# The first 230 microseconds of a delta-rule and feed-forward kernel: weight transfers, score blocks and one unit's keys in another order

## The chip, the cores and the metric

One core of one Trainium2 chip runs the kernel. The metric is device time in microseconds (us), the median of several runs; lower is better. The engines are called PE (TensorE, matmuls), DVE (VectorE), ACT (ScalarE), POOL (GpSimd) and SP (SyncE, which only issues transfers here).

## The reference, cut to what matters

The first half is a delta-rule recurrence for 4 batches (B), 8 heads (H), 768 positions (S) and head size 48 (D). Its output, with the heads side by side, is the input x (3072 rows of 384) of a feed-forward block with a hidden size of 2048.

```python
k_n = k / (np.linalg.norm(k, axis=-1, keepdims=True) + 1e-06)
for t in range(S):
    y[:, :, t] = np.einsum('bhd,bhde->bhe', q[:, :, t], state)
    v_old = np.einsum('bhde,bhd->bhe', state, kt)
    state = state + bt[:, :, :, None] * np.einsum('bhd,bhe->bhde', kt, vt - v_old)
...
h = x @ w_in
g = h * (1.0 / (1.0 + np.exp(-1.702 * h)))
return g @ w_out
```

The two weight matrices come as 64-bit floats and are made 32-bit on the chip.

## The kernel before, in words

**Units.** The sequence is cut into 6 chunks of 128 positions; a unit is one chunk of one batch with all 8 heads, so there are 24 units, units 0 to 3 in chunk 0, 4 to 7 in chunk 1, and so on. For each unit the keys are normalised (`normalize_mixed`, line 317: a square on ACT, a sum on DVE, a power on POOL, three instructions on DVE), turned (`turn`, 385: matmuls into psT, copied by ACT to kT), and their scores formed (`gram`, 362: matmuls into psG, copied by ACT to G). The 32-row diagonal blocks of the scores are written to a DRAM tile Nd and read back into NT so that each of 128 partitions holds one block (`prepare`, 389). `invert` (444) inverts these blocks for a whole chunk on DVE, from `NT*bI` (bI is beta) to YS; YS goes out to Yd in DRAM and comes back as XB. `Step` (538) then solves a unit in four blocks, one after the other: psU (solve, with XB), a copy of U on ACT, psR (below), a subtraction from V on DVE. A "hop" is one call of `together` (786) on two units in turn. `put_out` (951) forms the output psY, updates the state ST on DVE, and copies the output to xT. Part of each xT tile is moved between partitions by six small transfers `xT<-last` (681 to 690).

**Weights.** w_in is fetched in four quarters (`fetch_in`, 174, twelve transfers each, of 64 and 192 KB), w_out in 16 pieces (`fetch_out`, 190). They land in parts of tiles that are otherwise free (w_out's own space, gT, xT, M). `conversions` (255) turns them into 32-bit floats, five DVE instructions and one ACT instruction for a piece; each `fill(n)` puts n more of these instructions at its place in the program. Fetches of later pieces are tied to the end of a conversion (283 to 291): the end of piece ("in", 0, 1) calls fetch_in(3), the end of ("in", 1, 1) calls four fetch_out on POOL's queue.

**Order.** Engines and queues work in the order in which the program gives them. `pinned` (100) keeps an instruction in program order; `sync`, `beside` and `other_queue` (115) are such transfers on the queues of SP, ACT and POOL. What isn't pinned (`nc.sync.dma_start`) is placed by the scheduler. Each transfer on SP's and ACT's queues uses one of eight completion counters in turn, and waits for the counter's last user.

**The beginning (871 to 1031).** Keys of chunk 0 are normalised and turned, and only their diagonal blocks formed (`diagonal`, 428), for two units at a time; Nd is read back into NT as one transfer (913). Behind it stand on SP: QP and V of units 0 to 3, fetch_in(1) (half of it on POOL's queue), KN of units 4 to 6, fetch_in(2), and bI of the other chunks. `invert(0)` runs on DVE meanwhile; at its end `warm(NY)` puts 60 small matmuls on PE, and YS and XB go through DRAM. Then units 0 and 1 hop (973 to 978), with `warm(NU)` of 11 matmuls in each hop, are put out, and units 2 and 3 hop (998 to 1006), with the first hidden-layer matmuls (ph) from the fourth hop on. `keys` (956) prepares units 4 to 7 in 26 small steps among these hops, at steps 0, 3, 6 and 14; `ahead_of(preparing, n)` takes n steps. After chunk 0, `invert(1)` runs on DVE among ph matmuls. Then `woven` (828) is called for each unit, with the keys of the unit five ahead, so those of unit 8 in woven(3). `follow` (802) loads QP, KN and V for later units.

Of the kernel before, what the change touches and what calls it, by code (L numbers as in the profile page):

```python
# [18 lines left out]
def kernel(  # L19
# [19 lines left out]
    nc = tc.nc  # L39

    B, H, S, D = q.shape
# [8 lines left out]
    BS = 32  # L50
    NB = C // BS
    HB = 2
# [5 lines left out]
    NW, NA, NY, NU = 80, 3, 60, 11  # L58
# [20 lines left out]
    NT = cpool.tile([128, BS, BS], F32, name="NT")  # L79
# [4 lines left out]
    def load(n, pairs, dma=nc.sync.dma_start):  # L84
        c, b = units[n]
        for dst, src in pairs:
            dma(  # L87
                out=dst[n % len(dst)][:, :, 0:D],
                in_=src[b, :, c * C : (c + 1) * C, :].rearrange("h p d -> p h d"),
            )  # L90

    def load_values(n, dma=nc.sync.dma_start):
        c, b = units[n]
        V = io.tile([128, H, D], F32, tag="V", name="V", bufs=4)
        dma(
            out=V, in_=v[b, :, c * C : (c + 1) * C, :].rearrange("h p d -> p h d")
        )
        loaded[n] = V
# [33 lines left out]
    def warm(n, after=None):  # L132
        ps = ps_moe.tile([128, 256], F32, tag="moe", name="ps_warm")
        if after is not None:
            after(ps[:, 0:1], 0.0)
        for _ in range(n):
            pe.matmul(ps, lhsT=ones[:, 0:128], rhs=ones, start=True, stop=True)
# [36 lines left out]
    def fetch_in(i, other=None):  # L174

        f = slice(i * NQ, (i + 1) * NQ)
        raw = quarter(i if i < 3 else 4)
        for j in range(KC):
            for p, r, m, step in x_rows:
                (other if other and p >= DP else sync)(  # L180
                    out=as_rows(raw[j])[p : p + m, 0],
                    in_=moe_w_in[r + j * step : r + j * step + m, f],
                )
# [110 lines left out]
    def fill(n):  # L294
        for _ in range(n):
            next(converting, None)
# [92 lines left out]
    def prepare(n):  # L389

        c, b = units[n]
        turn(n)
        yield 0.6
        G = gram(n)
        if c == 1:
            Nd = dram.tile([H * C * BS], F32, tag="Nd", name="Nd", bufs=4)
            for blk in range(NB):
                u = slice(blk * BS, (blk + 1) * BS)
                sync(out=Nd.rearrange("(h p k) -> p h k", p=C, k=BS)[u], in_=G[u, :, u])
            yield 0.9  # L400
            sync(
                out=NT[b * NB * H : (b + 1) * NB * H].rearrange("d i k -> d (i k)"),
                in_=Nd.rearrange("(d r) -> d r", r=BS * BS),
            )
            yield 0.0
            return
        Nd = dram.tile([H * NS], F32, tag="Nd", name="Nd", bufs=4)
        dma = sync if c < 3 else nc.sync.dma_start
        dma(
            out=Nd.rearrange("(h r) -> h r", r=NS)[:, 0 : C * C].rearrange(  # L410
                "h (p k) -> p h k", k=C
            ),
            in_=G,
        )
        dma(
            out=NT[b * NB * H : (b + 1) * NB * H],
            in_=Nd.rearrange("(d r) -> d r", r=NS // NB)[:, 0 : BS * C].rearrange(
                "d (i k) -> d i k", k=C
            )[:, :, 0:BS],
        )  # L420
        yield 0.9
# [116 lines left out]
    class Step:  # L538
# [126 lines left out]
        def outputs(self, state=False):  # L665
            self.turned(
                (0, 4, 1, 5, 2, 6, 3, 7),
                lambda h: self.US[:, h * D : h * D + DP], lambda h: self.M[:, h, :],
                self.c == 0,
            )  # L670
            if state:
                self.state(self.psS)
            t = slice(self.b % HB * C, (self.b % HB + 1) * C)
            if t.start == 0:
                lasts[0] = wk.tile([128, NTH], F32, tag="o", name="last")
            last = lasts[0]
            act.copy(last[:, t], self.psY[1][:, 1, :])
            act.copy(self.xT[:, 0::2, t], self.psY[0])
            act.copy(self.xT[:, 1, t], self.psY[1][:, 0, :])

            if t.start > 0:
                t, dmas = slice(0, NTH), [nc.sync.dma_start] * 2
                if self.c == 0:
                    dmas = [sync, beside if self.b < HB else sync]
                for ct in range(2):
                    for j in range(KC):
                        dmas[ct](
                            out=self.xT[ct * DP + D : (ct + 1) * DP, j, t],
                            in_=last[ct * DP + j * XR : ct * DP + (j + 1) * XR, t],
                        )  # L690
# [74 lines left out]
    def ahead_of(work, n):  # L765
        for _ in range(n):
            next(work, None)
# [33 lines left out]

    def follow(n):

        if n + B < len(units):
            load(n + B, ((QP, q),))
        m = n - 1 + len(KN)
        if m < len(units):
            load(m, ((KN, k),), nc.gpsimd.dma_start)
        if n - 1 + B < len(units):
            load_values(n - 1 + B)  # L810
        if n % HB == 0 and n > B:
            h = (n - 1) // HB
            gT = []
            queue.append(hidden(xTs[h], gT, slice(0, NTH), 1.3))
            queue.append(written(*units[h * HB], gT))
            xTs.pop(h)
# [7 lines left out]
            debt[0] -= done  # L824

    STEPS = (9, 5, 3, 3, 3, 3)

    def woven(n, share):

        nonlocal inverting
        A, B_, D_ = steps.pop(n - 1, None), steps.get(n), steps.get(n + 1) or NoStep()
        m = n + B + 1
        K = (normalize if n > 6 else normalize_mixed)(m) if m < len(units) else iter(())
        P = prepare(m) if m < len(units) else iter(())
        if n % HB == 1 and B < n and n + 1 + HB < len(units):
            inverting = invert(*units[n + 1 + HB], HB)
        ahead = STEPS[:3] if n % HB == 1 else STEPS[3:]  # L840

        next(K, None)
        together([(B_, 1)], [(A, 2)])
        run(D_.scored)
        next(K, None)
        ahead_of(inverting, ahead[0])
        spend(share / 3)

        together([(A, 3), (D_, 0)], [(B_, 1)])
        next(K, None)  # L850
        ahead_of(inverting, ahead[1])
        spend(share / 6)
        next(P, None)
        spend(share / 6)

        together([(B_, 2)], [(D_, 0)])
        if A:
            A.queries()
            A.outputs(True)
        run(P)  # L860
        ahead_of(inverting, ahead[2])
        if n % HB == 0:
            run(inverting)
        spend(share / 6)
        next(new_step(n + 2).scored, None)
        spend(share / 6)
        follow(n)
# [34 lines left out]
    for b in range(B):  # L902
# [4 lines left out]
        if b % 2 == 1:  # L907
            for e in range(2):
# [1 line left out]
                    out=Nd.rearrange("(h e p k) -> e p h k", e=2, p=C, k=BS)[e, :, (b - 1) * NP : (b + 1) * NP],  # L910
                    in_=Ds[e][:, b - 1 : b + 1].rearrange("p b h j -> p (b h) j"),
                )
    sync(out=NT.rearrange("d i k -> d (i k)"), in_=Nd.rearrange("(d r) -> d r", r=BS * BS))
    pool.tensor_copy(landed, NT[:, 0, 0:1])
    for b in range(B):
        load(b, ((QP, q),), sync)
    for b in range(B):
        load_values(b, sync)
    fetch_in(1, other_queue)
    for n in range(B, len(KN)):  # L920
        load(n, ((KN, k),), sync)
    fetch_in(2)
    for blk in range(NB):
        sync(out=bI[blk::NB, 1:], in_=betas[:, 1:, blk, :])
    fill(6)
    for b in range(B):
        gram(b)
# [10 lines left out]
    run(inverting)  # L938
    for s in pair:
        s.select()  # L940
    fill(5)

    def hops(a, b):
# [12 lines left out]
    def keys():  # L956

        def unit(n):
            yield from normalize_mixed(n)
            yield from prepare(n)  # L960

        work = [unit(n) for n in range(B, 2 * B)]
        for t in range(26):
            for u, begin in enumerate((0, 3, 6, 14)):
                s = t - begin
                if s >= 0 and s % 2 == 0:
                    next(work[u], None)
            yield
        for w in work:
            run(w)  # L970
# [8 lines left out]
    for s in pair[:2]:  # L979
        put_out(s)  # L980
        fill(1)
        ahead_of(preparing, 1)
    load(7, ((KN, k),), sync)
    for n in range(B, B + 2):
        load(n, ((QP, q),), sync)
    for n in range(B, B + 2):
# [4 lines left out]
    def feed(n=1):  # L991
        for _ in range(n):
            while ffn and next(ffn[0], None) is None:
                ffn.pop(0)
# [4 lines left out]
    for i in range(2 * NB):  # L999
        together(*next(path))  # L1000
        if i > 2:
            feed()
        fill(2)
        ahead_of(preparing, 2)
        if 3 <= i < 6:
            fetch_out(i - 3)
# [5 lines left out]
    xTs.pop(0), xTs.pop(1)  # L1012
    run(preparing)
    load(B + 2, ((QP, q),), sync)
    load(8, ((KN, k),), sync)
    while not ("in", 3, 1) in done:
        fill(1)
    inverting = invert(1)
# [47 lines left out]
```

## Time and profile before

| | us |
|---|---|
| median of 3 runs | 798.52 (792.38 to 800.28) |
| profiled execution, its own time | 793.2 |
| its span | 791.4 |
| busy in the span: PE, DVE, ACT, POOL | 759.3, 458.7, 239.7, 127.6 |
| mean granted PE clock | 0.974 |

A row of the timeline reads: start, duration, engine, line, operation, output<-input, shape and count, and in brackets the idle time of the engine before it and what ended that. Nearly all instructions carry line 102, the helper that pins them, so they are told apart by the names of their tiles. "SPq" and "ACTq" are the engines' queues: the time is that of issuing, not of moving the data. A row of the table by stage reads: stretch, its length, busy time and count for PE, PE's weight loads, DVE, ACT and POOL, then the granted PE clock, the DMA engines' mean share and GB/s.

### The profile page before, as it was taken

The numbers are of one execution on the slowest core, as the hardware profiler recorded it, in microseconds if no ns is written. First come the engines' busy times: TensorE is split into PE (matmuls) and PEld (weight loads), VectorE is DVE, ScalarE is ACT, GpSimd is POOL, SyncE is SP. The second block draws the span as 40 slices with busy tenths as digits, with TensorE's granted clock in tenths as the row PEclk, the third lists the DMA queues.
The fourth block names the chain that finished last, engine by engine and source line by source line (L and its number), as shares of the span: only waits on it lengthen the run. The fifth ranks groups of instructions, "written<-read, shape, count | busy, mean of one in ns | idle before, by whom it ended". The sixth has DMA issues, their size and how long they took to land.

```text
span 791.4 us, 18653 instructions
## 1 busy us (share of the span) xinstructions
PE 759.3 (96%) x8068; PEld 568.7 (72%) x8068; DVE 458.7 (58%) x945; ACT 239.7 (30%) x521; POOL 127.6 (16%) x128
## 2 busy tenths in 40 slices
PE   9678899898899999999999999999999999999998
PEld 7467788654568768768768778678678678687684
DVE  5897669897996566656666756766756531100000
ACT  4433553234333323323223223223223123121110
POOL 4122220101221312212212212211210000000000
PEclk9689799989999999999999999999999999999999
DMA  6996752343323232232232232231230020000000
GB/s 125 158 176 136 152 138 58 75 135 84 81 49 90 54 77 51 55 86 42 59 79 45 62 87 43 52 99 27 60 82 11 22 44 2 12 15 1 25 1 20
DMA packets 139313, 52.81 MB, mean 67 GB/s; under 512 B 113808, under 2 KB 134416, under 8 KB 139232
## 3 DMA queue, kind: packets, MB, share of 16 engines
q1 hardware_dynamic: 136864, 43.65, 25.6%
q0 software_dynamic: 2176, 7.67, 3.7%
q8 instruction: 63, 1.03, 0.6%
q10 hardware_dynamic: 192, 0.31, 0.2%
q14 instruction: 18, 0.15, 0.1%
HBM read 33.13 MB, written 17.30 MB: 64 GB/s over the span
## 4 chain that ended last, share of the span: by engine, by line
PE 82%; DVE 9%; SPq 3%; DMA 3%; issue 1%; ACT 1%; ACTq 0%; POOL 0%; DVEq 0%; POOLq 0%
PE ph L102 29%; PE po L102 28%; PE psY L102 6%; PE psU L102 5%; PE psQ L102 3%; PE psG L102 3%; SPq L102 3%; PE ps_warm L102 2%; DVE w_out L102 2%; PE psT L102 2%; PE psR L102 2%; DVE tmp L102 2%; DVE P L102 1%; DVE V L102 1%; DVE YB L102 1%
## 5 line engine op out<-in xcount | busy, mean ns | idle before, releaser
L102 PE MATMUL po<-w_out,gT 128*128 128x384 f32 x768 | 267.1, 496 | 4.9 <-DVE w_out L102 4.8
L102 PE MATMUL ph<-xT,w_in 128*128 128x256 f32 x1152 | 262.8, 384 | 0.5 <-ACT gT L102 0.2
L102 PEld LDWEIGHTS ph<-xT,w_in 128*128 128x128 f32 x1152 | 215.5, 191 | 33.5 <-ACT gT L102 1.6
L102 PEld LDWEIGHTS po<-w_out,gT 128*128 128x128 f32 x768 | 141.8, 191 | 96.2 <-DVE w_out L102 7.2
L102 DVE TENSOR_TENSOR V<-V,psR 64x384 f32<-64x384 f32 (+1 forms) x96 | 53.3, 556 | 198.9 <-PE psR L102 197.7
L102 ACT ACTIVATE gT<-ph 128x512 f32<-128x512 f32 x96 | 56.4, 596 | 137.8 <-PE ph L102 137.6
L102 DVE TENSOR_TENSOR P<-NT,YB 64x8 f32<-64x8 f32 (+31 forms) x190 | 88.5, 466 | 5.3
L102 ACT COPY US<-psU 32x384 f32<-32x384 f32 x92 | 43.2, 470 | 143.0 <-PE psR L102 127.3
L102 PEld LDWEIGHTS psU<-V,XB 32*32 32x32 f32 x1536 | 59.3, 107 | 36.8 <-issue 27.4
L102 DVE TENSOR_REDUCE YB<-P 64x4 f32<-64x8 f32 (+31 forms) x190 | 80.9, 426 | 6.5
L102 PE MATMUL psU<-V,XB 32*32 32x48 f32 x1536 | 70.2, 205 | 2.1 <-DMA XB<-Yd 1.4
L598 POOL TENSOR_SCALAR_AFFINE_SELECT M<-M 128x1024 f32<-128x1024 f32 x20 | 26.1, 1307 | 245.5 <-DVE M L102 166.6
L102 PE MATMUL psR<-US,G 32*32 32x48 f32 x2208 | 61.4, 205 | 0.6 <-issue 0.6
L102 PEld LDWEIGHTS psR<-US,G 32*32 32x32 f32 x2208 | 51.9, 107 | 1.9 <-issue 1.9
L102 PE MATMUL ps_warm<-ident 128*128 128x256 bf16 x260 | 38.0, 301 | 11.7 <-ACT G L102 7.2
L102 PEld LDWEIGHTS <-ident 128*128 128x128 bf16 x260 | 26.5, 106 | 18.3 <-issue 11.2
L102 PE MATMUL psQ<-QS,kT 48*128 48x176 f32 (+1 forms) x384 | 34.8, 322 | 1.1 <-ACT QS L102 1.1
L102 PE MATMUL psG<-kT 48*128 48x128 f32 x384 | 32.4, 316 | 2.7 <-ACT kT L102 2.5
L102 DVE TENSOR_TENSOR P<-NT 64x256 f32<-64x256 f32 (+7 forms) x40 | 33.7, 843 | 0.3
L102 DVE TENSOR_REDUCE NT<-P 64x64 f32<-64x1024 f32 (+7 forms) x40 | 32.6, 815 | 1.4
L87 POOL DMA_DIRECT2D KN<-in_k_dram x15 | 14.2, 949 | 117.2 <-PE psY L102 108.2
L102 PEld LDWEIGHTS psQ<-QS,kT 48*128 48x128 f32 x384 | 28.6, 192 | 4.0 <-ACT QS L102 2.4
(96 smaller groups left out, 610.5 us busy)
## 6 DMA issues: line engine op xcount, KB each, us to landing
Nd<-G SPq DMA_DIRECT2D x16, 512.0 KB, 3.5
QP<-in_q_dram SPq DMA_DIRECT2D x24, 192.0 KB, 3.8
V<-in_v_dram SPq DMA_DIRECT2D x24, 192.0 KB, 2.9
out_dram<-o SPq DMA_DIRECT2D x24, 192.0 KB, 2.5
XB<-Yd SPq DMA_DIRECT2D x24, 128.0 KB, 3.3
KN<-in_k_dram POOLq DMA_DIRECT2D x15, 192.0 KB, 3.9
Yd<-YS SPq DMA_DIRECT2D x22, 128.0 KB, 2.5
NT<-Nd SPq DMA_DIRECT2D x20, 128.0 KB, 2.6
```

Of the source, the lines that this page charges most:

```text
L87: dma(out=dst[n % len(dst)][:, :, 0:D], in_=src[b, :, c * C : (c + 1) * C, :].rearrange("h p d -> p h d"),)
L102: return lambda *a, **kw: tc.keep_in_program_order(op(*a, **kw))
L598: (pool if self.n < B else nc.gpsimd).affine_select(out=self.M, in_=self.M, compare_op=ALU.is_gt, fill=0.0, base=0, pattern=[[0, H], [1, 1 ...
```

## The change

- fetch_in(1) moves behind the KN loads and bI; fetch_in(2) moves behind the end of `invert(0)`, its transfers and the selections of units 0 to 3.
- Nd of chunk 0 is read back into NT in two halves of 64 partitions, each after its pair of units.
- The six `xT<-last` transfers of units 0 and 1 all go on SP (three were on ACT).
- In put_out of units 0 and 1 no step of `keys` is taken any more. The first three hops of units 2 and 3 get `warm(NU // 2)`, 5 matmuls each.
- Unit 8 is added to `keys` at step 17: it is normalised and turned there; its gram and its transfers stay in woven(3), which takes the begun `prepare` from `begun`.
- KN of unit 8 is loaded together with that of unit 7, before QP and V of units 4 and 5. On SP the loads KN 7, KN 8, QP 4, QP 5, V 4, V 5 now stand between the first six xT transfers and the first Nd of chunk 1; the last NT of chunk 1 stands behind the second six xT transfers (before it was ahead of them).
- In `follow`, for n up to 4, the loads of QP and V are pinned.

```diff
@@ outputs
                 if self.c == 0:
-                    dmas = [sync, beside if self.b < HB else sync]
+                    dmas = [sync, sync]
@@ follow
+        dma = sync if n <= B else nc.sync.dma_start
         if n + B < len(units):
-            load(n + B, ((QP, q),))
+            load(n + B, ((QP, q),), dma)
...
         if n - 1 + B < len(units):
-            load_values(n - 1 + B)
+            load_values(n - 1 + B, dma)
@@ woven
+    begun = {}
...
+        if m in begun:
+            K, P = iter(()), begun.pop(m)
@@ beginning
-    sync(out=NT.rearrange("d i k -> d (i k)"), in_=Nd.rearrange("(d r) -> d r", r=BS * BS))
-    pool.tensor_copy(landed, NT[:, 0, 0:1])
+            d = slice((b - 1) * NB * H, (b + 1) * NB * H)
+            sync(
+                out=NT[d].rearrange("d i k -> d (i k)"),
+                in_=Nd.rearrange("(d r) -> d r", r=BS * BS)[d],
+            )
+    pool.tensor_copy(landed[64:], NT[64:, 0, 0:1])
...
-    fetch_in(1, other_queue)
     for n in range(B, len(KN)):
         load(n, ((KN, k),), sync)
-    fetch_in(2)
     for blk in range(NB):
         sync(out=bI[blk::NB, 1:], in_=betas[:, 1:, blk, :])
+    fetch_in(1, other_queue)
...
     for s in pair:
         s.select()
+    fetch_in(2)
     fill(5)
@@ keys
-        work = [unit(n) for n in range(B, 2 * B)]
+        begun[2 * B] = prepare(2 * B)
+
+        def first(n):
+            yield from normalize_mixed(n)
+            next(begun[n])
+
+        work = [unit(n) for n in range(B, 2 * B)] + [first(2 * B)]
         for t in range(26):
-            for u, begin in enumerate((0, 3, 6, 14)):
+            for u, begin in enumerate((0, 3, 6, 14, 17)):
@@ put_out of units 0 and 1, hops of units 2 and 3
         fill(1)
-        ahead_of(preparing, 1)
     load(7, ((KN, k),), sync)
+    load(8, ((KN, k),), sync)
...
         if i > 2:
             feed()
+        else:
+            warm(NU // 2)
...
     load(B + 2, ((QP, q),), sync)
-    load(8, ((KN, k),), sync)
```

## The prediction

> **What bounds the kernel now.** First the page's row of slices: TensorE (PE) is busy nearly everywhere after the first third, so what can be won lies in its holes and in its slow stretches, and both stand in the first 230 us.
>
> ```profile
> PE   9678899898899999999999999999999999999998
> DVE  5897669897996566656666756766756531100000
> PEclk9689799989999999999999999999999999999999
> ```
>
> Slices are 19.8 us. PEclk falls to 0.6 in the second (the first inversion, on DVE) and to 0.7 in the fifth. Then the timeline between 48 and 90 us, at the end of the first inversion:
>
> ```profile
> 54.06 1.23 DVE L102 TENSOR_TENSOR YS<-YB,bI 128x1024 f32<-128x1024 f32 x1
> 54.15 8.03 PE L102 MATMUL ps_warm<-ident 128*128 128x256 bf16 x60 [3.05 <-DVE ps_warm L102]
> 54.91 2.62 SPq L102 DMA_DIRECT2D bI<-in_beta_dram  x4
> ...
> 57.63 1.00 SPq L102 DMA_DIRECT2D Yd<-YS  x2
> 57.64 0.85 ACTq L102 DMA_DIRECT2D Yd<-YS  x2
> ...
> 60.13 2.85 SPq L102 DMA_DIRECT2D XB<-Yd  x4
> ...
> 63.60 0.86 PE L102 MATMUL psU<-V,XB 32*32 32x48 f32 x16 [1.43 <-DMA XB<-Yd]
> ```
>
> YS is ready at 54.06+1.23 = 55.29, but SP is still issuing bI and starts the write of YS 2.34 us later. PE, whose 60 warm matmuls end at 62.18, waits another 1.43 us for XB. The chain of waits agrees: from 25 to 57.6 us it is SP's queue. The timeline of ACT and of PE after the first two units:
>
> ```profile
> 85.23 1.88 ACTq L102 DMA_DIRECT2D xT<-last  x3
> 87.16 0.60 ACT L102 ACTIVATE kT<-psT 128x512 f32<-128x512 f32 x1 [1.79 <-issue]
> ```
> ```profile
> 87.81 2.08 PE L102 MATMUL psG<-kT 48*128 48x128 f32 x16 [2.04 <-ACT kT L102]
> ```
>
> ACT issues three transfers, so kT is late and PE stands for 2.04 us. The table by stage shows what follows:
>
> ```profile
> 84.00:86.00 2.00, 1.77 (x34) 1.41 (x30) 1.56 (x3) 0.79 (x4) 2.00 (x3) 1.00 0.25 39
> 88.00:90.00 2.00, 2.00 (x27) 1.78 (x31) 0.00 (x0) 0.19 (x2) 0.00 (x0) 0.50 1.01 364
> 98.00:100.00 2.00, 2.00 (x5) 1.58 (x6) 1.93 (x4) 0.86 (x2) 0.00 (x0) 0.50 0.63 128
> ```
>
> (last three columns: granted clock, DMA share, GB/s). The clock is 0.50 until about 101: the hole costs its 2.04 us and then slow matmuls. Last, DVE and SP around the second inversion:
>
> ```profile
> 122.25 1.22 DVE L102 TENSOR_TENSOR NT<-NT,bI 128x1024 f32<-128x1024 f32 x1
> ...
> 154.03 0.55 DVE L102 TENSOR_REDUCE ssq<-ksq 128x8 f32<-128x384 f32 x1 [2.25 <-ACT ksq L102]
> ```
> ```profile
> 115.48 0.31 SPq L102 DMA_DIRECT2D NT<-Nd  x1
> 116.92 4.29 SPq L102 DMA_DIRECT2D xT<-last  x6
> ```
>
> From 116.4 to 190 DVE has one idle of note, the 2.25 us before unit 8's ssq; PE waits for it (4.8 us for w_out, 2.3 for KN). So until 190 the end is carried by PE to 116, then by DVE.
>
> **The Trainium skill.** "TensorE: Matmul & The Clock Gate", Part 1, "What's actually happening": the array drops to half rate after an idle window of about 3.4 us and needs as long of busy time to return. The trace agrees on the halves, not the lengths: 2.04 us sufficed, and 13 us passed. "DMA: Bandwidth & Descriptors", "Issuing engines are not separate DMA queues": another issuing engine only saves sequencer time. The trace agrees: three xT transfers cost ACT 1.88 us and SP 2.20. The same page, "Anatomy of one DMA": about 2 us of a transfer are fixed; here a 32 KB block takes 1.9 us to land, 128 KB of NT 2.4 to 3.3.
>
> **The change part by part** (own time 793.2 us, span 791.4; the median shown is 798.5, so I subtract from both).
>
> *Start.* fetch_in(2), twelve transfers of 1.57 MB in all, goes behind XB, so YS leaves at once. What is left in front (QP, V, KN, bI, fetch_in(1): some 3.8 MB) is through by 25+3.8 MB/0.18 MB per us = 46. XB comes 2.3 us earlier, at about 61.2, but the 60 warm matmuls still end at 62.18: gain 1.4, not 2.3. The block matrix comes back in two halves: 512 KB took 24.96 to 28.68; 256 KB should take about 3.0 (between 2.6 for 128 KB and 3.7). Gain 0.7, less 0.1 since SP issues the first half ahead of the second pair of Nd writes, less 0 to 0.7 since these share the engines. DVE was idle 2.15 us before NT, so it can use it. Taken 0.3, ends -0.2 and +0.6. Sum: **-1.7**. SP's half of fetch_in(1) moves behind KN and bI; quarter 1 is first converted at 70, so its six issues may land 20 us later than 46: nothing. Quarter 2 is first converted at 79.91; from about 60 on, quarters 2 and 3 (3.1 MB at 0.19) are in by 77, before the xT rows at 84: no cost, with 3 us of cover on quarter 2's first third and more on the rest.
>
> *Second path of hops (84.9 to 111.6).* ACT's three issues go to SP: hole of 2.04 gone. psG of unit 4 and psT of unit 5 move behind the first hop, with warm matmuls in the first three hops: 15 of about 0.12 (11 took 1.31) = 1.7 us added on PE, part of it in waits that exist anyway. With no hole the clock should hold: PE was busy some 12 us of the 13 at half rate, 6 us at most to regain; the hops have a floor of 2.12 us (first path: 65.70, 67.82, 69.94) set by V on DVE, and KN of unit 6 (rn on POOL behind four fetch_out issues) holds V of hop 2 by about 1.5, so I take 5.0. Unit 8's psT adds 0.45; its four DVE instructions (0.55+0.17+0.20+0.56 = 1.48) and ksq meet DVE waits of 2.9+1.1 us there. Sum -2.04-5.0+1.7+0.5 = **-4.8**, ends -7 and -2.
>
> *SP after it.* In front of chunk 1's blocks now stand six xT (4.3), KN 7 and 8, two QP, two V. Their 1.18 MB with fetch_out's 1.57 MB should land by about 98, as before; then four rounds Nd, NT of 3.55 us (112.34 less 108.74 is 3.6) reach unit 7 by about 110. But the last NT is now issued behind the second six xT: psY end +0.84+4.29+0.1, +2.6 to land: 7.8 us after psY ends, where the inversion began 122.25-116.08 = 6.17 after. Behind that NT on SP stands only QP of unit 6, needed much later; behind the waiting instruction on DVE (NT times bI) stand the whole second inversion and all of w_out's conversions, for which PE waits. **+1.8**, ends 0 (if DVE's own conversions end later than assumed) and +4 (if the blocks are late too). Two waits on SP are new and cheap: KN 7 and 8 wait for the state matmuls of units 0 and 1, done before xT is issued, and the first half of NT waits for its own Nd pair, with the second pair (due 21.75, ready about 21.85) behind it.
>
> *Unit 8.* In the stretch bound by DVE its 1.48 us and the 2.25 us of idle before ssq go: **-3.7**. If PE's last ph ends late, the relu behind gT keeps up to 1.2 of it: ends -2 and -3.7. V 6 and 7 and QP 7 and 8, now in program order, now stand on SP behind the last raw fetch, which waits for a conversion that ends near 180; they are needed from 198 on and land 3 to 4 us after issue: nothing, with some 14 us of cover.
>
> Sum -1.7-4.8+1.8-3.7 = -8.4: own time 784.8, on the median **790.1**. After 190 PE has less idle left than before but DVE still leads to 226, so the gain should stay.
>
> **The rivals.**
> *More:* the hops regain the whole 6, the last NT isn't late, DVE needs no wait: -2.0-6.3-3.7, about -12: 786.5. For it: PE's matmuls alone, at full rate, fill the hops in about 19 us. Against: V and KN on DVE.
> *Less:* DVE's order (V, two conversions, KN steps: about 2.8 us a hop) replaces PE as the bound, or the clock falls again in some hole near the first ph, which waits for xT rows landing at about 91, the time it is due. Hops give -2, last NT +3: -1.7-2+3-3.7 = -4.4: 794.
> *Slower:* chunk 1's Nd writes wait behind seven loads on SP and each NT behind its own Nd; if the loads drain late, the second inversion, then all of DVE, starts late, 1 us per us. It decides from 10.2 us of lateness beyond the due time (the other terms sum to -10.2), NT of unit 7 landing after about 127. For it: in the page these 20 us were DMA's fullest, 1.38 to 1.43 around 94. Against: the loads landed by 99 although issued later. At 19 us: 807.
> *The edit does nothing:* XB still later than the warm row. Excluded by SP's order.
>
> **How the numbers follow.** Main 0.45 (own range 787 to 793), More 0.20, Less 0.23, Slower 0.12. One per cent, 8 us, is about what can be told here; the line is 790.5, inside Main. Faster: More and 0.28 of Main, 0.48; slower by over 1%: 0.10 of Slower; same: the rest, 0.42. Range 783 to 799.5: from More's far end over Less, with some us for the spread of the runs shown (792.4 to 800.3).
>
> **What would show it.** Yd issued within 0.2 us of YS, and psU released by warm, not by XB. No idle over 1 us on PE at 84 to 90 and clock 1.0 there; psY of unit 2 about 6.5 us earlier. NT of unit 7 issued behind xT, DVE idle 1 to 2 us before the second inversion. No ssq wait after it. A clock of 0.5 around 90 to 100, or NT of unit 7 after 120, would make it wrong.

## The result, and the profile after

| | before | changed |
|---|---|---|
| median, us (20 runs each, on one chip) | 796.67 (791.92 to 800.34) | 793.89 (789.08 to 799.36) |
| ratio of the times | | 0.9971 (95%: 0.9948 to 0.9994) |
| profiled execution: span, us | 791.4 | 795.0 |
| mean granted PE clock | 0.974 | 0.978 |

The change gives 0.29%, some 2.3 us, where 8.4 were forecast. The two profiled executions have it the other way round, each within its kernel's spread; a second profile of each (below) had spans of 801.2 and 790.8. So single spans aren't compared here; stretches between the same instructions are. (The profile of one kernel below, with three transfers on ACT again, is of an execution over 1.5% above that kernel's fastest; the ratios leave such executions out.)

The changed kernel's page, its slices (19.9 us each):

```profile
PE   9679999878899999999999999999999999999998
DVE  5796667998797656656666666666756530100000
PEclk9678899999999999999999999999999999999999
```

The clock's row reads 6, 7, 8, 8 in slices two to five, where it read 6, 8, 9, 7. Its timeline at the end of the first inversion (start, duration, engine, then the instruction):

```profile
55.79 1.23 DVE L102 TENSOR_TENSOR YS<-YB,bI 128x1024 f32<-128x1024 f32 x1
55.87 8.97 PE L102 MATMUL ps_warm<-ident 128*128 128x256 bf16 x60 [4.61 <-DVE ps_warm L102]
...
57.04 0.78 SPq L102 DMA_DIRECT2D Yd<-YS  x2
57.05 0.84 ACTq L102 DMA_DIRECT2D Yd<-YS  x2
...
59.16 2.82 SPq L102 DMA_DIRECT2D XB<-Yd  x4
...
64.77 0.86 PE L102 MATMUL psU<-V,XB 32*32 32x48 f32 x16
```

YS leaves 0.02 us after it is ready, and PE waits for no transfer: both as forecast. But YS is 1.7 us later than before, and the row of 60 took 8.97 us, not 8.03, so psU began 1.17 us later than before. SP's timeline around the second inversion, and DVE's:

```profile
120.22 1.96 SPq L102 DMA_DIRECT2D Nd<-G  x4
122.23 3.68 SPq L102 DMA_DIRECT2D xT<-last  x6
126.02 0.52 SPq L102 DMA_DIRECT2D NT<-Nd  x1
```
```profile
129.59 1.23 DVE L102 TENSOR_TENSOR NT<-NT,bI 128x1024 f32<-128x1024 f32 x1 [4.07 <-DMA NT<-Nd]
```

DVE stood 4.07 us for the last read into NT. The table by stage (length, busy time and count of PE, PE's weight loads, DVE, ACT, POOL; then clock, DMA share, GB/s):

```profile
66.00:72.00 6.00, 5.55 (x173) 4.38 (x172) 4.00 (x7) 1.60 (x5) 0.00 (x0) 1.00 1.04 238
72.00:78.00 6.00, 4.88 (x97) 3.73 (x97) 2.39 (x4) 2.29 (x4) 1.68 (x1) 0.68 0.72 187
78.00:84.00 6.00, 6.00 (x62) 4.10 (x62) 3.78 (x7) 0.47 (x1) 0.63 (x1) 0.50 0.08 17
84.00:90.00 6.00, 6.00 (x124) 5.36 (x121) 4.08 (x9) 3.70 (x9) 1.01 (x1) 0.96 0.01 3
96.00:102.00 6.00, 5.52 (x143) 4.25 (x143) 5.33 (x12) 3.64 (x7) 0.00 (x0) 1.00 0.97 230
```

The hole at 86 and its slow clock are gone, as forecast (clock 1.00 at 96 to 102). A new slow stretch lies in the first path, 74.2 to 84.4.

Stretches in us, between the same instructions: start of the first inversion (on DVE); first psU; from there to unit 0's copy of `last` (first path); from there to unit 3's (second path); from there to the start of the second inversion; from its YS to KN of unit 9.

| | inversion | psU at | first path | second path | to 2nd inversion | to KN 9 | span |
|---|---|---|---|---|---|---|---|
| before | 28.9 | 63.6 | 17.8 | 34.6 | 6.3 | 39.0 | 791.4 |
| before, second | 28.8 | 63.2 | 27.7 | 34.7 | 6.3 | 39.1 | 801.2 |
| changed | 30.6 | 64.8 | 23.3 | 31.1 | 10.4 | 35.6 | 795.0 |
| changed, second | 30.3 | 63.9 | 19.9 | 31.0 | 7.4 | 35.6 | 790.8 |

### The profile page after: what moved, and what is told of

Same layout as the page of the kernel before. It is cut to its first block, busy times and chain, and to the rows that moved or that the text cites. A ratio compares the mean times of both kernels' runs of the same rounds, so it can differ in the third digit from the quotient of the medians.

```text
span 795.0 us, 18695 instructions
## 1 busy us (share of the span) xinstructions
PE 759.3 (96%) x8083; PEld 567.4 (71%) x8083; DVE 459.0 (58%) x945; ACT 239.8 (30%) x521; POOL 123.3 (16%) x128
## 4 chain that ended last, share of the span: by engine, by line
PE 78%; DVE 14%; DMA 4%; issue 1%; ACT 1%; SPq 1%; DVEq 0%; POOL 0%; ACTq 0%; POOLq 0%
PE po L102 28%; PE ph L102 25%; PE psY L102 6%; PE psU L102 5%; DVE P L102 4%; PE ps_warm L102 3%; PE psQ L102 3%; DVE YB L102 3%; PE psG L102 3%; PE psT L102 2%; PE psR L102 2%; DVE w_out L102 2%; DVE NT L102 2%; DVE tmp L102 1%; SPq L102 1%
## 5 line engine op out<-in xcount | busy, mean ns | idle before, releaser
L102 PEld LDWEIGHTS po<-w_out,gT 128*128 128x128 f32 x768 | 140.7, 190 | 96.5 <-DVE w_out L102 8.0
L102 PEld LDWEIGHTS psU<-V,XB 32*32 32x32 f32 x1536 | 58.7, 107 | 34.6 <-issue 26.7
L102 PE MATMUL ps_warm<-ident 128*128 128x256 bf16 x275 | 44.4, 320 | 13.2 <-ACT G L102 7.2
L102 PEld LDWEIGHTS <-ident 128*128 128x128 bf16 x275 | 29.6, 113 | 22.0 <-issue 12.7
L102 PE MATMUL psG<-kT 48*128 48x128 f32 x384 | 30.5, 303 | 0.2
```

Of the source, the lines that this page charges most:

```text
L102: return lambda *a, **kw: tc.keep_in_program_order(op(*a, **kw))
```

## The experiments

Theory: the forecast's gains came where they were put, and were given back at three places that it priced wrongly (the halves of NT, the warm row, SP's order before the second inversion). Rivals: the weight fetch in the first path holds back PE's instructions and the clock; or it is all spread. Ratios are to the kernel before, with 95% intervals. The changed kernel's own are 0.9971 and, on another chip, 0.9979 (0.9951 to 1.0007). The intervals of five edits overlap these (NT in one transfer, unit 7's read ahead, the third quarter's fetch, unit 8, warm matmuls ahead of the row): there the ratio alone tells no gain or loss, and the stretches of the profiles decide.

### NT in one transfer again

```diff
-            d = slice((b - 1) * NB * H, (b + 1) * NB * H)
-            sync(
-                out=NT[d].rearrange("d i k -> d (i k)"),
-                in_=Nd.rearrange("(d r) -> d r", r=BS * BS)[d],
-            )
-    pool.tensor_copy(landed[64:], NT[64:, 0, 0:1])
+    sync(out=NT.rearrange("d i k -> d (i k)"), in_=Nd.rearrange("(d r) -> d r", r=BS * BS))
+    pool.tensor_copy(landed, NT[:, 0, 0:1])
```

> The changed kernel with chunk 0's blocks read back into NT as one transfer again; all else as changed. Theory 1 (the halves delay the second pair of blocks, since the first half's read stands between the two pairs of writes): the first inversion begins at about 28.9 us instead of 30.6, YS ends at about 55.3 instead of 57.0, the time falls by about 1.7 us. Rival (the 1.7 us are the spread of one profile): the inversion begins at 30 to 31 again, the time stays.

Measured: ratio 0.9942 (0.9911 to 0.9973), median 791.57. The inversion began at 28.91, YS ended at 55.32. SP's timeline of the changed kernel, then of this one:

```profile
21.63 0.49 SPq L102 DMA_DIRECT2D NT<-Nd  x1
22.21 0.54 SPq L102 DMA_DIRECT2D Nd<-blocks  x1
22.84 0.53 SPq L102 DMA_DIRECT2D Nd<-others  x1
26.47 0.47 SPq L102 DMA_DIRECT2D NT<-Nd  x1
```
```profile
21.79 0.36 SPq L102 DMA_DIRECT2D Nd<-blocks  x1
22.24 0.53 SPq L102 DMA_DIRECT2D Nd<-others  x1
25.00 0.34 SPq L102 DMA_DIRECT2D NT<-Nd  x1
```

With the first half's read in between, the last write is issued 0.6 us later and the read that follows it comes 3.63 instead of 2.76 us after it: 1.47 us, and the smaller read wins none of it back (issue to inversion 4.13 against 3.91). In all nine profiles with the halves, the later ones too, the inversion begins at 30.0 to 31.1, in the five without at 28.8 to 28.9. The theory holds for the start of the inversion; that the time falls by as much isn't shown by the ratio.

### Unit 7's read into NT ahead of the xT transfers

```diff
+    run(preparing)
     for s in pair[2:]:
         put_out(s)
```

> The changed kernel with the rest of the keys' steps run before units 2 and 3 are put out, so that unit 7's read into NT is issued ahead of the second six xT transfers. Theory 1 (the read waits for SP behind these six): the 4.07 us of DVE idle before the second inversion fall to about 1 to 1.5, since the read is issued about 2.5 us earlier; the time falls by 1 to 2.5 us. Rival (the blocks themselves are late, SP's order of the six is no matter): the idle stays at 3 to 4 us and the time too.

Measured: 0.9948 (0.9923 to 0.9972), median 791.99. SP's timeline and DVE's:

```profile
114.50 2.74 SPq L102 DMA_DIRECT2D Nd<-G  x4
118.52 0.31 SPq L102 DMA_DIRECT2D NT<-Nd  x1
118.88 3.69 SPq L102 DMA_DIRECT2D xT<-last  x6
```
```profile
122.97 1.22 DVE L102 TENSOR_TENSOR NT<-NT,bI 128x1024 f32<-128x1024 f32 x1
```

No idle is left before the second inversion, which begins 6.28 us after unit 3's copy of `last`, the same as before the change. In the nine profiles with this read behind the six, DVE waits 1.0 to 4.1 us for it; in the three with it ahead (two more below), 0.5 at most. The theory holds, and more idle than expected went.

### Fewer warm matmuls in the row

```diff
-    NW, NA, NY, NU = 80, 3, 60, 11
+    NW, NA, NY, NU = 80, 3, 40, 11
```

> The changed kernel with 40 instead of 60 warm matmuls at the end of the first inversion. Theory 1 (the warm row, no longer XB, ends last before the first solve): psU begins about 6.7 us after the warm row does instead of 8.9, released by XB, and the time falls by 1.5 to 2 us. Rival (XB lands no earlier than the row ends, about 3.4 us after its issue plus contention with the third quarter's fetch): psU begins where it did, with 2 us of PE idle before it, and the time stays or rises.

Measured: 0.9891 (0.9855 to 0.9928), median 788.67 of only 6 runs. The row took 7.02 us; psU began 6.95 after the row's start (8.90 in the changed kernel), still at the row's end and not after a wait. That XB would release it is missed; the row was what ended last, even with 40. The gain over the changed kernel's ratio, some 6 us, is more than 2: the one profile has no slow clock in the first path (18.6 us), and how much of the gain is the edit's stays open.

### The third quarter's fetch back in front of bI

```diff
         load(n, ((KN, k),), sync)
+    fetch_in(2)
     for blk in range(NB):
...
         s.select()
-    fetch_in(2)
```

> The changed kernel with the third quarter's fetch back in front of bI, all else as changed. Theory 1 (the move as such gives about nothing as long as the warm row ends last): YS is written 2 us after it is ready, psU is released by XB and begins 6 to 7.5 us after YS's end instead of 7.7, the time changes by less than 1 us. Rival theory 2 (the fetch, moved into the first path of hops, holds back PE's instruction fetch there, and the clock drops): with the fetch out of that stretch the idle of 1.57 us in the fourth hop is below 0.8 and the clock stays at 1.0 from 62 to 85, so the time falls by 2 to 5 us.

Measured: 0.9957 (0.9934 to 0.9981), median 793.67. Yd was written at 57.47, 0.31 us after YS, and psU began at the row's end, at 65.22, 8.1 us after YS, not released by XB: the fetch alone hardly held YS back here, because YS was late anyway. No gain or loss can be told. PE's idle in the fourth hop was 1.3 us and a slow stretch followed it, so the rival falls: it isn't this fetch's place alone that makes the idle.

### Both kernels once more

> The kernel before, once more, for a second profile. Theory 3 (run to run, it is mainly the TensorE clock's slow windows that differ, and the profile shown was one with few): the stretches between the same instructions agree within 0.5 us except where the clock is 0.5; the span is 2 to 5 us over 791.4 and the list of slow windows is longer. Rival: other stretches, without a slow clock, differ by over 1 us.

> The changed kernel, once more, for a second profile. Theory 3: the first inversion begins again at 30.6 to 31.1, the second after an idle of 3.5 to 4.5 us of DVE, the path from unit 2 to the end of chunk 0 takes again 31.1 us, and only the first path of hops (23.3 us in the first profile) differs, being 18.5 to 20.5 where the clock doesn't drop. Rival: it is 23 us again, so that the change itself drops the clock there.

Measured: 1.0016 (0.9977 to 1.0055) and 0.9979 (0.9951 to 1.0007). The second profile of the kernel before: PE's timeline and two rows of the table by stage.

```profile
63.23 1.48 PE L102 MATMUL psU<-V,XB 32*32 32x48 f32 x16 [2.47 <-DMA XB<-Yd]
```
```profile
66.00:72.00 6.00, 6.00 (x133) 4.27 (x135) 2.06 (x3) 0.47 (x1) 0.00 (x0) 0.50 1.02 210
78.00:84.00 6.00, 6.00 (x95) 4.36 (x93) 2.38 (x6) 0.47 (x1) 0.00 (x0) 0.50 0.01 3
```

Here the row ran at full clock, ended earlier, and the wait for XB was 2.47 us; the clock fell to 0.50 at 63.3 and stayed there for 24 us: the first path took 27.7 us, and the span was 9.8 us longer, not 2 to 5. All other stretches are within 0.4 us of the first profile's; the hole of 2.04 us in the second path is there again, with 13.7 us of half clock again. In the changed kernel the wait before the second inversion was 1.0 this time. SP's first two rounds from one read into NT to the next took 5.9 and 5.4 us in the first profile, 5.0 and 3.6 in this one; the six xT transfers started 3.1 us after unit 3's copy of `last` there, 1.0 here. So the idle was 1 us where the rounds were in time, and 3 more in the first profile: 2.1 from the later start of the six, 1.0 because the last read took longer from issue to use (3.57 against 2.59 us). The first path took 19.9 us with one short slow window. Theory 3 holds for both, but for that SP term.

### Three xT transfers on ACT again

```diff
-                    dmas = [sync, sync]
+                    dmas = [sync, beside if self.b < HB else sync]
```

> The changed kernel with three of units 0 and 1's six xT transfers on ACT's queue again. Prediction's theory (ACT's three issues make the hole of 2.04 us and with it the slow clock): ACT's copy of U for the first hop of units 2 and 3 comes 1.9 us later, PE idles about 1.5 us there, and the clock falls to 0.5 for about 10 us; time up 3 to 6 us. Rival (the hole was made by the order of psG and psT, which this kernel leaves changed, and the warm matmuls cover): idle under 1 us, clock 1.0, and SP's shorter list brings the second inversion's NT about 1.5 us earlier: time down 1 to 2 us.

Measured: 1.0064 (1.0038 to 1.0090), median 801.54. The table by stage:

```profile
88.00:92.00 4.00, 3.83 (x75) 2.79 (x76) 1.12 (x3) 1.66 (x4) 1.57 (x2) 0.51 0.99 328
92.00:100.00 8.00, 7.33 (x138) 6.19 (x139) 5.07 (x11) 3.35 (x6) 0.00 (x0) 0.50 0.66 150
100.00:120.00 20.00, 19.77 (x174) 14.59 (x173) 10.04 (x21) 8.01 (x14) 4.53 (x4) 0.53 0.78 139
```

PE stood 1.2 us for ACT's copy of G, the clock fell to 0.5 at 88.1, and PE, though busy, was at half clock for 31 us (this execution took 7 us more than the kernel's median, so that length isn't typical). On the same chip the changed kernel had 0.9979: the difference is 0.85%, some 7 us. The rival falls on the idle, the clock and the time. But the edit does more than it says. SP's timeline, and what SP waited for between 60 and 100 us (total, times, longest):

```profile
89.69 6.09 SPq L102 DMA_DIRECT2D w_out<-in_moe_w_in_dram  x8
```
```profile
SPq L102 <- DMA xT<-last: 18.6, 3, 17.1
```

ACT's three transfers take three of the eight completion counters in turn, and the fifth transfer of w_in's fourth quarter, next on SP, now waits for one of them to land. So eight of this quarter's twelve transfers leave at 89.7 to 95.8 (70.8 to 77.3 in the changed kernel), in the second path, and SP's own xT transfers only at 96.5. How much of the 7 us is ACT's hole with its clock, and how much this late fetch, was not separated.

### Unit 8 left where it was

```diff
-            for u, begin in enumerate((0, 3, 6, 14, 17)):
+            for u, begin in enumerate((0, 3, 6, 14)):
```

(`begun` and its work are left out too.)

> The changed kernel without unit 8 in the keys' steps, so that unit 8 is normalised and turned in the stretch after the second inversion as before. Prediction's theory: from YS of the second inversion to KN of unit 9 it takes 39.0 us again instead of 35.6, with DVE idle for about 2 us before unit 8's sum; the path of units 2 and 3 is shorter by 0.5 to 1; time up 2.5 to 3.5 us. Rival (PE, not DVE, sets the end there in the changed kernel): below 1 us.

Measured: 1.0018 (0.9987 to 1.0049), median 798.70. To KN of unit 9 it took 39.5 us, and DVE's timeline shows the wait again:

```profile
156.91 0.55 DVE L102 TENSOR_REDUCE ssq<-ksq 128x8 f32<-128x384 f32 x1 [2.67 <-ACT ksq L102]
```

In both profiles of the changed kernel this stretch was 35.6. PE's turning of unit 9, which waits for this KN, is later by as much, so the rival falls. The ratio on the same chip differs by 0.4%, some 3 us, which agrees, though the intervals overlap. The path of units 2 and 3 wasn't shorter (31.8 us, with a short slow stretch in it).

### Warm matmuls ahead of the row

```diff
+    warm(27)
     run(inverting)
     for s in pair:
```

> The changed kernel with 27 more warm matmuls on PE after unit 3's scores, where PE otherwise stands for 3 to 4.6 us before the row of 60. Theory 1 (that idle puts the row's first 3 to 7 us at half clock, so that the row, not XB, sets the first solve): the row of 60 takes 6.4 to 6.8 us instead of 8.4 to 9.5, psU begins 1.5 to 2.5 us earlier, now at or just after XB's landing; the clock is 1.0 from 44 on. Time down 2 to 3 us. Rival (clock windows fall as they like): the row takes over 8 us again.

Measured: 0.9941 (0.9914 to 0.9967), median 790.96. The row took 6.71 us with no slow clock, psU began at 62.31, 5.5 us after YS (7.75 in the changed kernel). It is still the row that ended last. The theory holds for the row and psU.

### The fetches held back until after the fourth hop

```diff
-        ("in", 0, 1): lambda: fetch_in(3),
...
+        if i == 3:
+            for j in range(KC):
+                vec.memset(homes[j].bitcast(F32)[:, 0:1], 0.0)
+            fetch_in(2)
+            fetch_in(3)
```

> The changed kernel with the fetches of w_in's third and fourth quarters held back until after the fourth hop of units 0 and 1, by a small write of DVE into the third quarter's place; a look only, since they then collide with the xT rows. Theory 2 (PE's idle of 0.6 to 1.6 us in the fourth hop is its instruction fetch, which waits among the weight transfers): with no other transfer under way there the idle falls below 0.4. Rival: it stays at 0.6 or more, so it isn't the load of the DMA engines. Total time up by 2 to 8 us in either case.

Measured: 1.0030 (1.0007 to 1.0053), median 799.02. Whom PE waited for between 62 and 92 us (engine, line, releaser, total, times, longest), in the changed kernel and here:

```profile
PE psR L102 <- issue: 1.6, 1, 1.6
```
```profile
PE psT L102 <- ACT G L102: 0.7, 1, 0.7
```

The idle in the fourth hop is gone, not only smaller. With weight transfers under way it was 0.6 to 2.7 us in twelve of the other thirteen profiles; the exception is the second of the kernel before, whose PE ran at half clock there. With none under way it is nil. It has moved with the fetches: in the second path, where they now run, PE stands again without a wait:

```profile
94.16 0.28 PE L102 MATMUL psU<-V,XB 32*32 32x48 f32 x1 [2.14 <-issue]
```

The trace's DMA records show what precedes these holes. In every one of the twelve profiles with the idle in the fourth hop, a transfer of 16 KB on an instruction queue ended 1.3 to 1.5 us before PE went on (in the changed kernel it ran from 70.57 to 71.81, and the idle ended at 73.12); for the hole at 94.16 above it is 1.4 us. With weight transfers under way these took 1.2 to 1.4 us there; in this kernel, up to the end of the first path, 0.88 to 0.95. The queue has 63 such transfers in the whole kernel, one for some 240 of PE's instructions. So that PE's instructions come late is the likeliest reading; the records don't name the engine. The full time went up: in the profile PE's clock fell at 93.4, during that hole, and PE then stood 3.1 us for xT rows, whose transfers met the fetches.

### Three edits together

NT in one transfer, `run(preparing)` ahead, and a row of 40:

> The changed kernel with three things together: NT as one transfer, unit 7's read into NT ahead of the second xT transfers, a row of 40 instead of 60 warm matmuls. Theory 1: the parts add up, first inversion at 28.9, psU at 60.5 to 61, no idle of DVE before the second inversion; relative to the changed kernel 1.7 + 2 + 2 = 5 to 6 us less. Rival (PE idles for XB and the clock falls in the first path): psU at 61 with over 1.5 us of idle, and the first path takes 21 us or more.

The same with the row of 60 and `warm(27)` ahead of it:

> As the kernel with three things together, but with the row of 60 kept and 27 warm matmuls put in front of it. Theory 1: row at full clock from 54.1 to 60.6, XB at about 60.9, psU there, and a first path without slow clock of 18 to 19 us; time at or 1 to 2 us below the kernel with the shorter row. Rival: same as the kernel with the shorter row within 1 us, since that one has little slow clock left.

Measured: 0.9889 (0.9842 to 0.9936), median 787.24, and 0.9892 (0.9838 to 0.9947), median 787.07, six runs each. The profile of the first drew an idle of 2.7 us in the fourth hop and then six slow windows (first path 27.8 us, span 792.6); its psU had begun at 60.3. That of the second has no slow clock between 47 and 158 (span 784.2). Its PE timeline and DVE's waits:

```profile
51.54 10.00 PE L102 MATMUL ps_warm<-ident 128*128 128x256 bf16 x90
61.47 0.86 PE L102 MATMUL psU<-V,XB 32*32 32x48 f32 x16
```
```profile
DVE V L102 <- PE psR L102: 7.5, 6, 1.9
DVE ST L102 <- PE psY L102: 4.6, 3, 3.0
DVE NT L102 <- DMA xT<-last: 0.5, 1, 0.5
```

PE now runs without a stop into psU, and DVE's wait for NT is 0.5. Both versions beat both kernels by about 0.8 to 1.1%; between them no difference can be told.

## Why the prediction was wrong

The direction was right and the time lies inside the range, but the sum of 8.4 us was 6 too large. By its steps:

**Start, -1.7: wrong in sign, and the largest miss.** YS left at once, as said. (a) The halves were taken at a gain of 0.3, with a loss of 0.2 as the worst end. They cost 1.4 to 1.7. The step that failed is the price of the first half's read between the two pairs of writes: put at 0.1, it took 1.5 (the last write 0.6 later, the read behind it another 0.9). And the half as a transfer took no less than the whole, where the forecast scaled the landing with the bytes. (b) The warm row was taken to end at 62.18 as before. It starts with the inversion's end, which moved by 1.7, and its length was read as fixed, although the quoted 8.03 us held some slow clock: 60 matmuls took 6.7 to 9.5 us. A later inversion also leaves PE idle for longer ahead of the row, 3.5 to 4.8 us with the halves where it was 3.05, and 3.4 to 5.7 us of the row then ran at half clock, where it was 2.7; where warm matmuls filled that idle, the row took 6.71. So psU came at 63.9 to 64.8 instead of 61.9.

**The first path, put at nothing.** The forecast asked of the two fetches there only whether they land in time, and gave them "no cost". PE's idle in the fourth hop (0.64 us in the profile of before, overlooked) was 1.3 and 1.6 in the changed kernel's two profiles, and a slow stretch followed both times. Held-back fetches remove the idle; putting back the third quarter's alone doesn't, so the size isn't the work of that move alone, and whether the change makes it larger on average stays open. Idle and clock together made the first path 5.5 us longer in the first profile and 2.1 in the second; that isn't the change's alone, since the kernel before lost 9.9 there in its second.

**Second path, -4.8: -3.5.** The hole and its slow clock went, as forecast: both profiles of the kernel before have 2.04 us of hole and 13.7 us of half clock there, the changed kernel's two no hole over 0.7 us and no half clock. What that was worth alone (forecast 2.04 and 5.0) isn't shown, since the experiment with ACT also held back a fetch; so whether the clock was priced too high or the additions (warm matmuls, unit 8) too low stays open.

**SP, +1.8: +1.1 to +4.2.** The mechanism was right: the last NT stands behind the six xT. (Its own figures, 7.8 less 6.17, give 1.6.) The rounds of Nd and NT were taken at 3.55 us; they took 3.6 to 5.9, and in the first profile even the fourth Nd was late, so that NT of unit 7 was issued at 126.0, past the 120 that the forecast named as a sign of being wrong (119.6 in the second). This is the first part of the rival "slower", at a small size.

**Unit 8, -3.7: -3.45**, and 3.9 in the stretch of the experiment. Right.

Together: +0.3 to +1.2, some +0.8 for the idle, -3.5, +1.1 to +4.2, -3.45 is -0.8 to -4.8, around the measured -2.3; the first path's slow clock, which comes and goes in both kernels, is not in this sum. Of the rivals "less" came nearest, -4.4 with its term for the last NT. That its 794 is the measured median is luck: the kernel before had 796.67 in these runs, not 798.5. Its reasons for the hops, DVE's order or a clock that falls near the first ph, were not seen, and it had the same wrong start of -1.7.

## What to carry to other kernels

A transfer split in halves need not be half as long (here 4.13 us from issue to use, against 3.91 for the whole): look at what stands between the halves in its queue, here writes that the second half itself waits for. A filler sized to cover a wait becomes the bound once the wait is shortened; size it anew together with the edit, and read its length together with the clock it ran at. Before pricing a gain in single microseconds, take two profiles: stretches without a slow clock mostly agreed to 0.4 us here, spans differed by up to 10. And an experiment that puts one thing back can move another: look at every queue of its trace before its time is read as the price of that one thing.

## What the runs showed of the hardware that was not expected

The TensorE clock falls after short holes and in some runs only: 2.47 us of idle brought 24 us at half clock in one run of the kernel before, 1.43 us brought none in another. In the fourth hop a slow stretch began during the idle or within 2 us of it in six of the seven profiles where it was 1.27 us or longer, and in none of the five where it was 1.1 or less. The slow stretches between 20 and 230 us came in steps of about 3.4 us (3.4, 6.8, 10.2, 13.7, 17.1, 20.5, 23.9, 30.7), which agrees with the window of that length that the Trainium skill gives in "TensorE: Matmul & The Clock Gate", "What's actually happening". What differs is how long a busy PE stayed slow: 24 and 31 us at a busy share of over 0.9.

And PE, without any wait that the profile shows, stood for 0.6 to 2.7 us while the DMA engines were full, at the same place of the program in twelve of fourteen profiles, each time until 1.3 to 1.5 us after a 16 KB transfer on an instruction queue had ended.
